# One token of gated attention plus a GLU: the first loads divided over two issue queues

## The chip, the cores and the metric

The kernel runs on one core of a Trainium2 chip. Five engines work side by side, each with its own instruction queue: TensorE (PE) for matmuls, VectorE (DVE), ScalarE (ACT), GpSimd (POOL) and SyncE (SP). Sixteen DMA engines move data between the chip's memory (HBM) and the on-chip memory of 128 partitions (SBUF). A load is issued by an instruction in the queue of SP, ACT or POOL and ends by raising a semaphore. The metric is device time in microseconds (us), the median of several runs.

## The reference

One token attends to the last 4096 positions of a cache with 8 key/value heads and 32 query heads; a small network with a sigmoid runs beside it; a scalar gate mixes the two.

```python
W = min(4096, max(256, Sk // 4))               # 4096
q = (x @ wq).reshape(B, Sq, Hq, Dh)            # x: 512, wq: 512 x 4096
k, v = (last W positions of k_cache, v_cache)  # 8 heads x 4096 x 128 each
p = softmax(q . k * Dh ** -0.5)
a = (p . v).reshape(B, Sq, Hq * Dh) @ wo       # wo: 4096 x 512
h = sigmoid(x @ w_gate) * (x @ w_up)           # 512 x 1792 each
b = h @ w_down                                 # 1792 x 512
g = sigmoid((x * gate_w).sum(-1))
out = g * a + (1 - g) * b
```

All inputs are bf16. Each weight and each cache row is used once, and together they are 30.7 MB.

## The kernel before

All large loads are issued by SP in the order in which they are used: `wq_sb` (L80, 4 MB, 32 KB per partition), the four K pairs `kn` (L84 through `load_pair`, 2 MB each), `wg_sb` (L94), `wu_sb` (L99) and its remainder `wx_sb` (four small loads, L105), the four V pairs `vv`, `wo_sb` in two halves (L115) and `wd_sb` in four pieces (L120), the last of them 128 KB. A pair is two heads of the cache, and partition 2x + y of its tile holds head y's block number x. The V pairs take over the buffers of the K pairs, so that each V load waits until the K pair's transposes are done. `wo_sb` takes over the buffer of `wq_sb`.

ACT issues two small loads at the very start: x and `gate_w`, 1 KB each, into one partition of `xr` (L74, L75). At the end it issues the output (L343).

POOL makes the constants: `identf`, `ident`, `ones_f`, the zeroed `qbig`, `permT` (L123 to L134). DVE clears a scalar `spare` four times (L137), makes `other` and `selI`, and forms the gate from `xr` (gpr L165, gsum L166, then z_ps L168 on PE and gex L170 on ACT). PE turns x into a column (`xt_ps` L148, copied to `xT` L158).

From L177 on the order on PE, DVE and ACT is the order of the program text; before it, and on SP and POOL, the framework's scheduler sets it. PE first fills the score tiles with a mask (L182), then computes q, replicated over all partitions, in eight pieces of four matmuls (`q_ps` L200). ACT copies each piece (L202), DVE transposes (`qtT` L205) and places q in `qbig` (L216). For each of four pairs and two halves DVE transposes K in 32 x 32 blocks (`kT` L188) and PE adds eight matmuls to the scores (L227). Then come the maximum, the gate matmuls of the GLU (`glu(0)`), the exponential (L269), its transpose `eT` (L271), the 64 matmuls with V (`pv_ps` L299), the up matmuls (`glu(1)`), the reordering of the attention result (`oT`, `oX`, `oY`), and 92 narrow pairs' worth of matmuls with `wo_sb` and `wd_sb` that add everything into `a_ps` (`add_row`, L290). DVE and ACT copy the result (L341, L342).

The framework gives loads issued by SP and ACT eight completion semaphores in rotation. A load whose semaphore still belongs to an unfinished load waits in its queue, and everything behind it in that queue waits with it. The end of the program (L369) is a chain of waits on SP for every semaphore that is still open, and then a meeting of all engines.

Of the kernel before, what the change touches and what calls it, by code (L numbers as in the profile page):

```python
# [17 lines left out]
def kernel(  # L18
# [14 lines left out]
    nc = tc.nc  # L33

    P = 128
# [7 lines left out]
    W = min(4096, max(256, Sk // 4))  # L43
    KB = W // P
    SBASE = Sk - W
# [3 lines left out]
    NC_O = HQ * DH // P  # L49
# [5 lines left out]
    HP = Hkv // 2  # L55
    R2 = 2 * REP
    NP = 2 * KB
# [13 lines left out]


    xr = const.tile([1, 2, D], BF16, name="xr")
    nc.scalar.dma_start(xr[:, 0, :], A_x[0, :, :])  # L74
    nc.scalar.dma_start(xr[:, 1, :], gate_w.rearrange("(o n) -> o n", o=1))  # L75

    dq = nc.sync
    wq_sb = big.tile([P, DC, HQ * DH], BF16, name="wq_sb", tag="big")
    wq_v = A_wq.rearrange("(p c) n -> p c n", c=DC)
    dq.dma_start(wq_sb[:], wq_v)  # L80


    def load_pair(t, cache, a, n0=0, n1=NP):
        dq.dma_start(t[:, n0:n1, :].rearrange("p n d -> p (n d)"),  # L84
                     cache[0, 2 * a:2 * a + 2, SBASE:SBASE + W, :]
                     .rearrange("y (x n) d -> x y n d", n=NP)[:, :, n0:n1, :].rearrange("x y n d -> x y (n d)"))

    kn = []
    for a in range(HP):
        kn.append(blk.tile([P, NP, P], BF16, name="kn", tag="blk"))  # L90
        load_pair(kn[a], A_k_cache, a)

    wg_sb = w14.tile([P, DC, F], BF16, name="wg_sb", tag="w14")
    dq.dma_start(wg_sb[:], B_w_gate.rearrange("(p c) f -> p c f", c=DC))  # L94
# [13 lines left out]
    for a in range(HP):  # L108
        vv.append(blk.tile([P, NP, P], BF16, name="vv", tag="blk"))
        load_pair(vv[a], A_v_cache, a)  # L110

    wo_sb = big.tile([P, NC_O, N_OUT], BF16, name="wo_sb", tag="big")
    wo_v = A_wo.rearrange("(p c) n -> p c n", c=NC_O)
    for c0 in (0, NC_O // 2):
        dq.dma_start(wo_sb[:, c0:c0 + NC_O // 2, :], wo_v[:, c0:c0 + NC_O // 2, :])  # L115

    wd_sb = w14.tile([P, NJ, N_OUT], BF16, name="wd_sb", tag="w14")
    wd_v = B_w_down.rearrange("(p j) n -> p j n", j=NJ)
    for j0, j1 in zip(WD_SPLIT[:-1], WD_SPLIT[1:]):
        dq.dma_start(wd_sb[:, j0:j1, :], wd_v[:, j0:j1, :])  # L120


    identf = const.tile([P, P], F32, name="identf")  # L123
# [9 lines left out]
    nc.gpsimd.tensor_copy(permT[:].rearrange("p (k j) -> p k j", j=4),  # L133
                          ident[:].rearrange("p (j k) -> p k j", j=4))  # L134
    spare = const.tile([1, 1], F32, name="spare")
    for _ in range(4):
        nc.vector.memset(spare[:], 0.0)  # L137

    other = const.tile([2, HQ * 4 // R2, 2, REP], BF16, name="other")
# [234 lines left out]
```

## Time and profile before

| quantity | value |
|---|---|
| median of 6 runs | 80.47 us (80.29 to 80.73) |
| the profiled execution | 80.44 us, of which 78.8 us span |
| busy PE, DVE, ACT, POOL | 53.7, 38.9, 10.8, 3.3 us |
| HBM read | 30.67 MB, 389 GB/s over the span |
| x's first consumer (DVE L153, PE L148) | 2.04 to 2.06 us |
| gate_w's consumer (DVE L165) | 8.01 us |
| first query matmul (L200) | 13.34 us |
| last load's first consumer (L290) | 75.62 us |
| mean granted TensorE clock | 0.957 |

The slices of the page divide the span into 40 equal parts; a digit is a busy share in tenths. The chain is read backwards from the last instruction: what released it, what released that, and so on. A waits line gives who waited for whom, with the total, the number of times and the longest. A windows line gives the stretch and its length, then the busy time and number of instructions of PE, its weight loads, DVE, ACT and POOL, then the granted clock, the mean share of the 16 DMA engines and GB/s. In a window that is shorter than a packet's time the DMA figures count the packets that begin in it, so that a share can exceed 1.

### The profile page before, as it was taken

Reading aid. Unit: us, or ns where it says so; the run is one execution under the profiler, and the core shown is the slowest. Engines: PE = TensorE matmul, PEld = TensorE weight load, DVE = VectorE, ACT = ScalarE, POOL = GpSimd, SP = SyncE. Lnnn points to the kernel's source line nnn. Section 1 sums busy time; section 2 is a strip of 40 time slices with the busy share of each in tenths; the row PEclk is TensorE's granted clock in tenths of the full one; section 3 lists DMA queues with packets and bytes.
Section 4 is the critical chain, followed back from the end, with each engine's and each line's share of the span. In section 5 each row is a group of like instructions: output and inputs, shape, how many; then the busy total and the mean of one; then the engine's idle time right before and its main releaser. Section 6 shows DMA issues by size and latency. Waiting matters only on the chain.

```text
span 78.8 us, 798 instructions
## 1 busy us (share of the span) xinstructions
PE 53.7 (68%) x314; PEld 24.1 (31%) x314; DVE 38.9 (49%) x52; ACT 10.8 (14%) x20; POOL 3.3 (4%) x10
## 2 busy tenths in 40 slices
PE   0200093999960999988889511999998799566750
PEld 0200041333410334433333110344442345345520
DVE  1600920009739999999995618994000000690020
ACT  2400000233763000000000257000000002000010
POOL 7900000000000000000000000000000000000000
PEclk9999999999999579999999999569999999999999
DMA  5889988999999999999999999999999999999710
GB/s 150 299 349 516 433 383 374 416 466 433 416 416 449 441 408 416 447 400 440 396 444 426 416 416 458 433 424 399 424 449 441 416 408 441 428 383 414 284 38 1
DMA packets 2616, 30.71 MB, mean 390 GB/s; under 512 B 307, under 2 KB 438, under 8 KB 822
## 3 DMA queue, kind: packets, MB, share of 16 engines
q1 hardware_dynamic: 2608, 30.67, 92.7%
q8 instruction: 2, 0.03, 0.2%
q10 hardware_dynamic: 6, 0.00, 0.0%
HBM read 30.67 MB, written 0.00 MB: 389 GB/s over the span
## 4 chain that ended last, share of the span: by engine, by line
DMA 76%; PE 13%; DVE 6%; ACT 1%; issue 0%
DMA wd_sb<-in_B_w_down_dram 36%; DMA vv<-in_A_v_cache_dram 24%; DMA wq_sb<-in_A_wq_dram 16%; PE q_ps L200 12%; DVE kT L188 3%; DVE qbig L216 2%; DVE qtT L205 1%; PE a_ps L290 1%; ACT q_sb L202 1%; DVE res L341 1%
## 5 line engine op out<-in xcount | busy, mean ns | idle before, releaser
L227 PE MATMUL S_ps<-kT,qbig 128*128 128x512 bf16 x64 | 16.3, 406 | 3.9 <-DVE qbig L216 2.8
L188 DVE STREAM_TRANSPOSE kT<-kn 128x2048 f32<-128x2048 f32 x8 | 17.8, 2279 | 0.0
L299 PE MATMUL pv_ps<-vv,eT 128*32 128x512 bf16 x64 | 15.2, 411 | 3.6 <-DVE eT L271 2.8
L227 PEld LDWEIGHTS <-qbig 128*128 128x128 bf16 x64 | 6.5, 103 | 13.7 <-issue 4.4
L200 PE MATMUL q_ps<-wq_sb,xT 128*128 128x512 bf16 x32 | 9.6, 475 | 1.4 <-DMA wq_sb<-in_A_wq_dram 1.4
L299 PEld LDWEIGHTS <-eT 128*32 128x32 bf16 x64 | 6.0, 103 | 11.9 <-issue 3.6
L205 DVE STREAM_TRANSPOSE qtT<-q_sb 128x512 f32<-128x512 f32 x4 | 2.8, 701 | 7.9 <-ACT q_sb L202 7.9
L318 DVE TENSOR_TENSOR oT<-o_ps,rb 128x32 bf16<-128x32 f32 x1 | 0.2, 191 | 12.1 <-PE o_ps L316 12.1
L200 PEld LDWEIGHTS <-xT 128*128 128x128 bf16 x32 | 3.8, 118 | 7.6 <-issue 5.5
L182 PE MATMUL S_ps<-ident,other 2*128 2x512 bf16 x4 | 2.0, 611 | 5.9 <-DVE other L140 5.9
L202 ACT CAST q_sb<-q_ps 128x512 bf16<-128x512 f32 x8 | 4.7, 585 | 8.0 <-PE q_ps L200 8.0
L290 PE MATMUL a_ps<-wo_sb,oY 128*1 128x256 bf16 x64 | 3.8, 272 | 1.7 <-DMA wo_sb<-in_A_wo_dram 1.4
L290 PEld LDWEIGHTS <-oY 128*1 128x1 bf16 x64 | 2.7, 83 | 3.3 <-issue 1.6
L271 DVE STREAM_TRANSPOSE eT<-e_sb 128x1024 bf16<-128x1024 bf16 x2 | 2.4, 1224 | 1.9 <-ACT e_sb L269 1.9
L254 ACT ACTIVATE sge<-gu_ps 128x448 f32<-128x448 f32 x1 | 0.5, 543 | 18.9 <-PE gu_ps L243 18.9
L165 DVE TENSOR_TENSOR gpr<-xr 1x512 f32<-1x512 bf16 x1 | 0.7, 679 | 4.7 <-DMA xr<-in_gate_w_dram 4.7
L341 DVE CAST res<-a_ps 1x256 bf16<-1x256 f32 x1 | 0.4, 412 | 5.2 <-PE a_ps L290 5.2
L281 DVE RECIPROCAL sg<-sge 128x448 f32<-128x448 f32 x1 | 3.0, 2953 | 0.0
L309 ACT COPY pv_sb<-pv_ps 128x512 f32<-128x512 f32 x1 | 0.6, 585 | 16.6 <-PE pv_ps L299 16.6
L249 DVE TENSOR_REDUCE pm<-S_ps 128x1 f32<-128x1024 f32 x2 | 2.4, 1204 | 0.9 <-PE S_ps L227 0.9
L148 PE MATMUL xt_ps<-ident,xr 1*128 1x1 bf16 x4 | 0.3, 165 | 3.5 <-POOL ident L126 3.5
L290 PE MATMUL a_ps<-wd_sb,hT 128*1 128x256 bf16 x28 | 2.0, 271 | 0.7 <-DMA wd_sb<-in_B_w_down_dram 0.7
(62 smaller groups left out, 31.0 us busy)
## 6 DMA issues: line engine op xcount, KB each, us to landing
kn<-in_A_k_cache_dram SPq DMA_DIRECT2D x4, 2048.0 KB, 27.5
vv<-in_A_v_cache_dram SPq DMA_DIRECT2D x4, 2048.0 KB, 18.8
wq_sb<-in_A_wq_dram SPq DMA_DIRECT2D x1, 4096.0 KB
wo_sb<-in_A_wo_dram SPq DMA_DIRECT2D x2, 2048.0 KB
wg_sb<-in_B_w_gate_dram SPq DMA_DIRECT2D x1, 1792.0 KB
wu_sb<-in_B_w_up_dram SPq DMA_DIRECT2D x1, 1456.0 KB
wd_sb<-in_B_w_down_dram SPq DMA_DIRECT2D x1, 1024.0 KB
wd_sb<-in_B_w_down_dram SPq DMA_DIRECT2D x1, 384.0 KB
```

What stands on the lines that cost most here:

```text
L182: nc.tensor.matmul(S_ps[u // 2][:, u % 2, :], lhsT=other[:].rearrange("p o y u -> p (o y u)"), rhs=ident[0:2, 0:2].rearrange("p (o y) -> p ...
L188: nc.vector.transpose(t[:].bitcast(F32), kn[a][:, v * KB:(v + 1) * KB, :] .rearrange("p n d -> p (n d)").bitcast(F32))
L200: nc.tensor.matmul(q_ps[:], lhsT=xT[:, c:c + 1].to_broadcast([P, P]), rhs=wq_sb[:, c, ks], start=(c == 0), stop=(c == DC - 1))
L202: nc.scalar.copy(q_sb[:, ks], q_ps[:])
L205: nc.vector.transpose(qtT[:].bitcast(F32)[:, kq], q_sb[:].bitcast(F32)[:, kq])
L216: copy(q_dst[rows, :, 32 * qd:32 * qd + R2, :, t], q_src[rows, :, :, :, 0, t])
L227: nc.tensor.matmul(S_ps[v][:, hb, :], lhsT=q_st[:, a, dhi, :, t], rhs=k_v[:, hb * 16:(hb + 1) * 16, dhi, :, t], start=False, stop=(a == HP ...
L249: nc.vector.tensor_reduce(pm2[:, v:v + 1], S_ps[v][:].rearrange("p a b -> p (a b)"), axis=AX.X, op=ALU.max)
L271: nc.vector.transpose(eT[:, :, v * KB:(v + 1) * KB, :].rearrange("p a n r -> p n a r"), e_sb[:, v, :].rearrange("p (n a r) -> p n a r", a= ...
L281: nc.vector.reciprocal(sg[:], sge[:])
L290: nc.tensor.matmul(a_ps[32 * i:32 * i + 1, i, 0:HN], lhsT=lhsT, rhs=rhs[:, i * HN:(i + 1) * HN], start=start, stop=stop)
L299: nc.tensor.matmul(pv_ps[32 * a:32 * a + 32, :, :], lhsT=eT[:, a, 4 * m:4 * m + 4, :].rearrange("p n r -> p (n r)"), rhs=vv[a][:, 4 * m:4 ...
```

## The change

The load of `wq_sb` becomes two: the even partitions by SP's queue, the odd ones by ACT's. The first three K pairs are divided in the same way, which sends the one head of a pair by SP and the other by ACT; the fourth stays whole on SP, like everything behind it. x and `gate_w` are issued by GpSimd instead of ACT. SP gets a no-operation behind its last load, which depends on the last eight loads in the list. DVE clears `spare` twice instead of four times.

```diff
     xr = const.tile([1, 2, D], BF16, name="xr")
-    nc.scalar.dma_start(xr[:, 0, :], A_x[0, :, :])
-    nc.scalar.dma_start(xr[:, 1, :], gate_w.rearrange("(o n) -> o n", o=1))
+    nc.gpsimd.dma_start(xr[:, 0, :], A_x[0, :, :])
+    nc.gpsimd.dma_start(xr[:, 1, :], gate_w.rearrange("(o n) -> o n", o=1))
 
     dq = nc.sync
+    loads = []
+    queues = (dq, nc.scalar)
     wq_sb = big.tile([P, DC, HQ * DH], BF16, name="wq_sb", tag="big")
     wq_v = A_wq.rearrange("(p c) n -> p c n", c=DC)
-    dq.dma_start(wq_sb[:], wq_v)
+
+    for y, queue in enumerate(queues):
+        queue.dma_start(wq_sb[y:P:2], wq_v[y:P:2])
 
     def load_pair(t, cache, a, n0=0, n1=NP):
-        dq.dma_start(t[:, n0:n1, :].rearrange("p n d -> p (n d)"),
...
+        loads.append(dq.dma_start(t[:, n0:n1, :].rearrange("p n d -> p (n d)"),
...
     for a in range(HP):
         kn.append(blk.tile([P, NP, P], BF16, name="kn", tag="blk"))
-        load_pair(kn[a], A_k_cache, a)
+        if a == HP - 1:
+            load_pair(kn[a], A_k_cache, a)
+            continue
+        for y, queue in enumerate(queues):
+            queue.dma_start(kn[a][y:P:2, :, :].rearrange("p n d -> p (n d)"),
+                            A_k_cache[0, 2 * a + y, SBASE:SBASE + W, :].rearrange("(x n) d -> x (n d)", n=NP))
...
-        dq.dma_start(wo_sb[:, c0:c0 + NC_O // 2, :], wo_v[:, c0:c0 + NC_O // 2, :])
+        loads.append(dq.dma_start(wo_sb[:, c0:c0 + NC_O // 2, :], wo_v[:, c0:c0 + NC_O // 2, :]))
...
-        dq.dma_start(wd_sb[:, j0:j1, :], wd_v[:, j0:j1, :])
+        loads.append(dq.dma_start(wd_sb[:, j0:j1, :], wd_v[:, j0:j1, :]))
+
+    seen = dq.nop()
+    for load in loads[-8:]:
+        tc.add_manual_dep(seen.ins, load.ins.name,
+                          mybir.DependencyInfo(mybir.DependencyClass.Sync, mybir.DependencyReason.DATA), reason="loads ended")
...
     spare = const.tile([1, 1], F32, name="spare")
-    for _ in range(4):
+    for _ in range(2):
         nc.vector.memset(spare[:], 0.0)
```

More of the change, by code (lines that the diff above doesn't have):

```diff
@@ L73 @@
     xr = const.tile([1, 2, D], BF16, name="xr")
-    nc.scalar.dma_start(xr[:, 0, :], A_x[0, :, :])
-    nc.scalar.dma_start(xr[:, 1, :], gate_w.rearrange("(o n) -> o n", o=1))
+    nc.gpsimd.dma_start(xr[:, 0, :], A_x[0, :, :])
+    nc.gpsimd.dma_start(xr[:, 1, :], gate_w.rearrange("(o n) -> o n", o=1))
     dq = nc.sync
+    loads = []
+    queues = (dq, nc.scalar)
     wq_sb = big.tile([P, DC, HQ * DH], BF16, name="wq_sb", tag="big")
     wq_v = A_wq.rearrange("(p c) n -> p c n", c=DC)
-    dq.dma_start(wq_sb[:], wq_v)
+    for y, queue in enumerate(queues):
+        queue.dma_start(wq_sb[y:P:2], wq_v[y:P:2])
     def load_pair(t, cache, a, n0=0, n1=NP):
-        dq.dma_start(t[:, n0:n1, :].rearrange("p n d -> p (n d)"),
-                     cache[0, 2 * a:2 * a + 2, SBASE:SBASE + W, :]
-                     .rearrange("y (x n) d -> x y n d", n=NP)[:, :, n0:n1, :].rearrange("x y n d -> x y (n d)"))
+        loads.append(dq.dma_start(t[:, n0:n1, :].rearrange("p n d -> p (n d)"),
+                                  cache[0, 2 * a:2 * a + 2, SBASE:SBASE + W, :]
+                                  .rearrange("y (x n) d -> x y n d", n=NP)[:, :, n0:n1, :].rearrange("x y n d -> x y (n d)")))
     kn = []
```

## The prediction

> **What bounds the kernel now.** I read the page's slices first, then its DMA queues, the chain of work that ended last, and at last the waits and windows around the two ends of the load stream.
>
> ```profile
> PE   0200093999960999988889511999998799566750
> DVE  1600920009739999999995618994000000690020
> DMA  5889988999999999999999999999999999999710
> GB/s 150 299 349 516 433 383 374 416 466 433 416 416 449 441 408 416 447 400 440 396 444 426 416 416 458 433 424 399 424 449 441 416 408 441 428 383 414 284 38 1
> q1 hardware_dynamic: 2608, 30.67, 92.7%
> q8 instruction: 2, 0.03, 0.2%
> q10 hardware_dynamic: 6, 0.00, 0.0%
> ...
> DMA 76%; PE 13%; DVE 6%; ACT 1%; issue 0%
> ```
>
> The DMA row stands at 9 from the fourth or fifth slice to the 37th: the 16 engines are full while PE and DVE have holes. The 30.67 MB of q1 fill 92.7% of 78.8 us, 73.0 us on each engine. So the end is the start of the load stream, plus 73 us, plus what follows the last load.
>
> The chain in order of time says the same of the end:
>
> ```profile
> 0.73 12.56 DMA wq_sb<-in_A_wq_dram
> 13.34 9.61 PE q_ps L200 x32
> ...
> 28.07 18.81 DMA vv<-in_A_v_cache_dram
> 46.90 28.68 DMA wd_sb<-in_B_w_down_dram
> 75.62 0.64 PE a_ps L290 x6
> 76.26 0.40 DVE res L341
> ```
>
> The last load is consumed from 75.62 us on; 0.64 us of matmuls, the 0.40 us copy, the output's transfer and the closing waits make 3.2 us up to 78.8. The profiled run took 80.44 us, so 1.64 us lie outside the span; the median is 80.47, 0.03 above. The piece at 28.07 is a V load waiting in line behind other loads, not an idle queue.
>
> Compute has little slack against the loads, in four waits (the last line is from SP's own waits; columns: who for whom, us in total, times, longest):
>
> ```profile
> PE q_ps L200 <- DMA wq_sb<-in_A_wq_dram: 1.4, 1, 1.4
> PE pv_ps L299 <- DMA vv<-in_A_v_cache_dram: 0.9, 1, 0.9
> PE a_ps L290 <- DMA wo_sb<-in_A_wo_dram: 1.4, 1, 1.4
> PE a_ps L290 <- DMA wd_sb<-in_B_w_down_dram: 0.7, 2, 0.5
> DVE gpr L165 <- DMA xr<-in_gate_w_dram: 4.7, 1, 4.7
> SPq L105 <- DMA wq_sb<-in_A_wq_dram: 8.3, 1, 8.3
> ```
>
> The reader is to see two numbers here: 1.4 us before the query matmuls, and 0.9 + 1.4 + 0.7 = 3.0 us later, which a late compute chain can eat before the end moves.
>
> The start, in narrow windows (columns: window, busy of the engines, clock, DMA share, GB/s booked where a packet starts):
>
> ```profile
> 0.00:1.70 1.70, 0.00 (x0) 0.00 (x0) 0.24 (x4) 0.18 (x1) 1.15 (x8) 1.00 0.00 1
> 1.70:2.10 0.40, 0.00 (x0) 0.04 (x1) 0.06 (x1) 0.40 (x1) 0.40 (x1) 1.00 3.92 1065
> 2.10:2.40 0.30, 0.00 (x0) 0.07 (x1) 0.30 (x2) 0.30 (x1) 0.30 (x1) 1.00 0.00 0
> 2.40:2.60 0.20, 0.00 (x0) 0.00 (x0) 0.20 (x2) 0.20 (x1) 0.20 (x1) 1.00 1.35 492
> ```
>
> 0.40 us x 1065 GB/s is 13 packets of 32 KB, one on each of 13 engines; 0.20 x 492 is the three others, about 0.6 us later (middles of the windows: 1.9 and 2.5). That stagger, and not a lack of queued work, is what a second queue could shorten.
>
> **The change, part by part.** *wq and three K pairs as halves on two queues.* Bytes stay (10.5 MB); five instructions' work becomes nine: SP issues one wq half, three K halves and the fourth pair; ACT four halves. Rows for one issue: 0.39 us (wq) and 0.61 to 0.74 us (K). On ACT four of them replace two small ones (0.51 and 0.21 us): its queue is busy to 0.73 + 0.39 + 3 x 0.68 = 3.2 us instead of 1.5, then its table load of 1.28 us ends at 4.5 instead of 2.8. ACT's first work is gex at 10.72; over 6 us cover it. Without them the gate chain would move one for one.
>
> The gain at the start: if a half of wq spreads over the 16 engines in half the time, the 0.6 us stagger shrinks to 0.3. Bounds: 0.6 us saved, and 0.3 lost if two queues that start together delay each other (an estimate: half of the 0.7 us by which the first packets, about 1.9 us, exceed the usual 1.21). I take -0.3, the middle of none and all of the stagger. More cannot be had here, since the stream behind runs full: DMA shares of 1.01 and 1.02 in the windows from 13.34 to 61.63. Four more loads end with 16 completion packets each, one per engine, of 9 ns: +0.04 us.
>
> [...]
>
> *Does a second queue's ring cost?* No row shows two bulk queues on one engine. The nearest are two. gate_w's 1 KB packet went between wq's packets at 6.4 us and no wq packet around it was longer: 0. The instruction fetch (two packets of 16 KB, 1.06 and 1.11 us) did cost: the V packet behind the first took 1.11 us instead of 0.61, the packet behind the second 0.76 instead of 0.31, so 0.5 us for a bulk switch. Each engine has 32 packets in the two-queue phase; alternating after every packet would make up to 32 x 0.5 = 16 us. A gain is bounded by the packets too: 32 KB take 1.213 us and twice 16 KB 2 x 0.614, so a packet costs 15 ns beside its bytes; a second ring that hid it for 32 packets would save 0.5. Ends: -0.5 and +16. I take 0, because gate_w went by a queue of the same kind as these loads (hardware_dynamic, q10) and the fetch by another (q8), and keep 16 for a rival.
>
> *Do the halves still use all 16 engines, evenly?* Nearest row: wx's loads of 32 partitions, whose packets were never more than nine in flight, mostly eight. A half on eight engines would move 10.5 MB at 213 instead of 427 GB/s: +24.6 us. Below: 0. I take 0, because wx's source is divided into eight blocks, and the halves have 64 equal rows in source and target.
>
> [...]
>
> *SP's order.* The trace shows eight completion semaphores in rotation: the ninth load reuses the first one's. That is the wait of L105 for wq above. Now the first eight are the two wq halves and six K halves, so the fourth K pair waits for wq (about 13.3 us), and wg, wu and wx, which are behind it on SP, wait each for a K half. At 13.3 us 6.3 MB are still queued, 14.8 us of work; at the thinnest point, about 26.6 us, 5.6 MB (fourth K pair, wg, wu, wx), 13 us. So 0; if that cover ran out, idle DMA time would add itself to the end. V loads wait as before for the K tiles' transposes (first at 28.07).
>
> *x and gate_w by GpSimd.* Two issues leave ACT and go ahead of POOL's seven constants. Bounds for one from ACT's rows and POOL's longest: 0.21 to 1.86 us, so `ident` is ready between 3.9 and 7.2 us instead of 3.4. The consumer is xt_ps, which then waits for x anyhow. The arrival matters more. Before, x arrived at 2.04, ahead of wq's packets, but gate_w, behind three of them, at 8.01. From there gpr, gsum, the constants and L182's matmuls take 4.0 us (8.01 to 11.99), and wq lets q_ps start at 13.34: gate_w may arrive up to 9.4 us. With two bulk rings ahead, I put x at 6.4 to 9 us, and gate_w one round of two 32 KB packets (2.5 us) after the first packet at 6.4: 8.9. Bounds 8.0 and 13.8 (three rounds). The value stays within the 1.4 us; 13.8 makes q_ps 4.4 us late, and 3.0 us of that disappear in the later waits: +1.4 at the end.
>
> *SP's no-operation* waits for the last eight loads. Behind it on SP is only the kernel's closing chain of waits, which already waits there (23.4 us for wd, with longest 21.8). With it, the output's own semaphore can be followed by few others; the closing waits after the output cost about 0.06 us each. 0, bounds -0.1 and +0.2.
>
> *Two memsets fewer on DVE*: 2 x 0.06 us and gaps, before x arrives. 0, below which nothing can come since DVE then waits for x; above, 0.35 us (selI) if the constants change places with the gate chain.
>
> **Sum:** 80.44 - 0.3 + 0.04 = 80.18 against the profiled run; with the 0.03 to the median, 80.2.
>
> **Rivals.** *Nothing moves*: the stagger stays, since all first packets end near 3.7 to 4.4 us whatever their start; 80.5. For it: full DMA rows. Against it: the last engine to finish also fixes the end.
>
> [...]
>
> *x too late*: gate_w after 12.4 us (9.4 + 3.0) moves the end; 80.5 to 82.0 (13.8 - 12.4 = 1.4 over 80.5). For it: 4.7 us waited already. Against: the three later waits.
>
> **How the numbers follow.** Tell-apart bound for this kernel: 0.3%, 0.24 us. Start gain: 0.58, its own range 79.8 to 80.8 (0.6 saved and 0.1 at the tail, or 0.3 lost), of this 0.40 faster, 0.14 same, 0.04 slower. Nothing moves: 0.12 (0.09 same, 0.03 slower). Rings or halves cost: 0.18, slower. x late: 0.12, slower. Faster 0.40, same 0.23, slower 0.37. The range goes from 79.5 (the start's 79.8 with part of the hidden 15 ns) to 82.4 (late x at its bound of 82.0, the tail's 0.2 and 0.2 more if wq lands later); it leaves out most of the ring case, 0.15, and 0.03 below.
>
> **What would show it.** Right: packets of all 16 engines before 2.3 us, DMA share near 1.0 from 4 us, the wait for wd near 75.4 us. K landings at 18, 23, 28 and 33 us as before. Wrong: a mean GB/s under 400 between 4 and 26 us (rings, halves); q_ps released by DVE and not by wq, with no wait left on wo or wd (x late); new waits on SP after the output's landing (tail); an idle DMA slice after 13 us (semaphore rotation).

## The result and the profile after

| quantity | before | after |
|---|---|---|
| median of all runs | 80.46 us (35 runs) | 80.95 us (16 runs) |
| median of the runs that the ratio uses | 80.44 us (27 runs) | 80.86 us (9 runs) |
| ratio, with its 95% interval | | 1.0051 [1.0039, 1.0063] |
| the profiled execution | 80.44 us | 80.86 us |
| its span, and what lies outside it | 78.78 + 1.66 us | 79.13 + 1.73 us |
| first packets of `wq_sb` begin | 1.75 us | 2.09 us |
| gate_w's consumer | 8.01 us | 13.89 us |
| first query matmul | 13.34 us | 17.86 us |
| last load's first consumer | 75.62 us | 75.94 us |

The change makes the kernel 0.5% slower, 0.41 us. Some executions of most versions were disturbed and took about 1.3 us or more longer; the ratios leave them out, and of the profiles of four experiments that fell in such an execution (split only, columns, adjacent blocks, no-operation only) only the first 23 us and the closing are read.

The two profiled executions differ by 0.42 us, and the table says where: 0.32 us in the moment at which the last load is consumed, 0.08 us outside the span, and the remaining 0.02 in the closing. So the question is why the load stream ends 0.32 us later. The page of the kernel after shows no hole in the stream and no lost bandwidth (slices of the DMA engines, then the queues, with packets, MB and share):

```profile
DMA  0999897999999999999999999999999999999710
...
q1 hardware_dynamic: 2352, 25.43, 76.1%
q10 hardware_dynamic: 322, 5.24, 16.3%
...
q0 software_dynamic: 64, 0.00, 0.1%
```

5.24 MB have moved to ACT's queue (q10), and the two shares, 76.1 and 16.3%, make 92.4% of 79.1 us, where q1 alone had 92.7% of 78.8 before: 73.1 us per engine against 73.0. The first slice of the DMA row has fallen from 5 to 0, though. The windows at the start show the same more finely (columns as in the prediction):

```profile
1.70:2.10 0.40, 0.00 (x0) 0.00 (x0) 0.00 (x0) 0.00 (x0) 0.40 (x2) 1.00 0.65 164
2.10:2.40 0.30, 0.00 (x0) 0.00 (x0) 0.00 (x0) 0.00 (x0) 0.30 (x2) 1.00 4.05 1092
2.40:2.60 0.20, 0.00 (x0) 0.00 (x0) 0.00 (x0) 0.00 (x0) 0.20 (x2) 1.00 0.45 164
2.60:3.60 1.00, 0.00 (x0) 0.00 (x0) 0.00 (x0) 0.34 (x1) 0.98 (x3) 1.00 0.30 98
```

The last column times the length gives the 32 KB packets that begin: 0.40 x 164 is two, 0.30 x 1092 is ten, 0.20 x 164 one, 1.00 x 98 three. Before, 13 began in the first of these windows. The stream is the same one, shifted by about a third of a microsecond.

The chain of work that ended last has a new head and the old tail:

```profile
1.84 12.02 DMA xr<-in_gate_w_dram
...
17.86 9.47 PE q_ps L215 x32
...
48.25 27.64 DMA wd_sb<-in_B_w_down_dram
75.94 0.65 PE a_ps L305 x6
76.58 0.40 DVE res L356
```

At its head stands `gate_w` instead of `wq_sb`: 12.02 us for 1 KB. The compute chain really starts 4.5 us later (q_ps at 17.86 instead of 13.34). But the tail still hangs on the load of `wd_sb`, as before. The waits say how close that was (who for whom, us in total, times, longest):

```profile
PE xt_ps L163 <- DMA xr<-in_A_x_dram: 10.9, 1, 10.9
...
DVE gpr L180 <- DMA xr<-in_gate_w_dram: 2.7, 1, 2.7
...
PE a_ps L305 <- DMA wd_sb<-in_B_w_down_dram: 0.2, 1, 0.2
```

Of the waits for loads that the kernel before had later on, the ones before `q_ps`, the V matmuls and `wo_sb` are gone. 0.2 us before the last piece of `wd_sb` is all that remains: the 4.5 us were absorbed, to within that margin. SP's own waits hold what the change does to the completion semaphores:

```profile
SPq L88 <- DMA wq_sb<-in_A_wq_dram: 8.4, 1, 8.4
```

The fourth K pair now waits for a wq half, as the prediction had it, and the full DMA row shows that it starved nothing.

### The profile page after: what moved, and what is told of

Its sections match the earlier page's. It is cut to its first block, busy times and chain, and to the rows that moved or that the text cites. A ratio compares the mean times of both kernels' runs of the same rounds, so it can differ in the third digit from the quotient of the medians.

```text
span 79.1 us, 805 instructions
## 1 busy us (share of the span) xinstructions
PE 52.3 (66%) x314; PEld 23.6 (30%) x314; DVE 37.8 (48%) x50; ACT 10.8 (14%) x20; POOL 4.4 (6%) x12
## 3 DMA queue, kind: packets, MB, share of 16 engines
q1 hardware_dynamic: 2352, 25.43, 76.1%
q10 hardware_dynamic: 322, 5.24, 16.3%
## 4 chain that ended last, share of the span: by engine, by line
DMA 50%; DVE 16%; PE 15%; issue 10%; SPq 3%; ACT 1%; POOL 1%; DVEq 0%; POOLq 0%
DMA wd_sb<-in_B_w_down_dram 35%; DMA xr<-in_gate_w_dram 15%; PE q_ps L215 12%; DVE kT L203 11%; PE S_ps L197 2%; DVE qbig L231 2%; SPq L124 1%; SPq L129 1%; DVE qtT L220 1%; DVE gpr L180 1%; DVE gsum L181 1%; PE a_ps L305 1%; ACT q_sb L217 1%; SPq L88 1%; POOL xr L74 1%
## 5 line engine op out<-in xcount | busy, mean ns | idle before, releaser
L242 PE MATMUL S_ps<-kT,qbig 128*128 128x512 bf16 x64 | 16.3, 405 | 3.9 <-DVE qbig L231 2.8
L314 PE MATMUL pv_ps<-vv,eT 128*32 128x512 bf16 x64 | 14.2, 412 | 2.8 <-DVE eT L286 2.8
L242 PEld LDWEIGHTS <-qbig 128*128 128x128 bf16 x64 | 6.4, 102 | 13.8 <-issue 4.5
L314 PEld LDWEIGHTS <-eT 128*32 128x32 bf16 x64 | 5.8, 103 | 10.3 <-DVE eT L286 2.9
L284 ACT ACTIVATE e_sb<-S_ps,nb 128x1024 bf16<-128x1024 f32 x2 | 2.2, 1109 | 0.0
```

What stands on the lines that cost most here:

```text
L242: nc.tensor.matmul(S_ps[v][:, hb, :], lhsT=q_st[:, a, dhi, :, t], rhs=k_v[:, hb * 16:(hb + 1) * 16, dhi, :, t], start=False, stop=(a == HP ...
L284: nc.scalar.activation(e_sb[:, v, :], S_ps[v][:].rearrange("p a b -> p (a b)"), AF.Exp, bias=nb[:], scale=scale, accum_out=rs2[:, v:v + 1])
L314: nc.tensor.matmul(pv_ps[32 * a:32 * a + 32, :, :], lhsT=eT[:, a, 4 * m:4 * m + 4, :].rearrange("p n r -> p (n r)"), rhs=vv[a][:, 4 * m:4 ...
```

## The experiments

Three candidates were there for the late start: that two queues which start a bulk load at the same moment delay each other; that a load of 64 partitions takes longer to issue, whatever its queue; and that x by GpSimd is at fault, by its lateness or otherwise. The issue instructions of the two kernels pointed at the second (start, us, engine, line, operation). Before:

```profile
0.73 0.39 SPq L80 DMA_DIRECT2D wq_sb<-in_A_wq_dram  x1
```

After:

```profile
0.73 0.56 SPq L84 DMA_DIRECT2D wq_sb<-in_A_wq_dram  x1
0.74 0.54 ACTq L84 DMA_DIRECT2D wq_sb<-in_A_wq_dram  x1
1.23 0.62 POOL L74 DMA_DIRECT2D xr<-in_A_x_dram  x1 [0.79 <-POOLq L373]
```

Half as many rows take 0.17 us more. But these two instructions also run side by side, so the trace alone couldn't tell the first two candidates apart.

### Only x and gate_w by GpSimd

The kernel before with this edit alone:

```diff
-    nc.scalar.dma_start(xr[:, 0, :], A_x[0, :, :])
-    nc.scalar.dma_start(xr[:, 1, :], gate_w.rearrange("(o n) -> o n", o=1))
+    nc.gpsimd.dma_start(xr[:, 0, :], A_x[0, :, :])
+    nc.gpsimd.dma_start(xr[:, 1, :], gate_w.rearrange("(o n) -> o n", o=1))
```

> The kernel before, with x and gate_w issued by GpSimd and nothing else changed. Theory S (two bulk queues that issue their first loads at the same moment slow each other, so the stream starts about 0.3 us later): SP issues wq alone in about 0.39 us, first packets near 1.75 us, last load consumed near 75.6 us, 80.3 to 80.5 us. Theory X (x's late arrival sets the end): gate_w's consumer after 12 us, q_ps near 16 to 18 us, no wait left on wo, 80.8 to 81.0 us.

Measured: 1.0026 [1.0016, 1.0037], the profiled execution 80.68 us. The load stream is untouched: `wq_sb` issues in 0.38 us, first packets at 1.75, the last load consumed at 75.62 as before. gate_w's consumer moves to 10.56 and the first query matmul to 14.47 us, and the waits for `wo_sb` (1.2 us) and `wd_sb` (0.8) stay: the lateness of x costs nothing here. The 0.24 us between the two profiled executions are elsewhere. 0.06 lie outside the span (1.72 instead of 1.66), 0.05 before the output has landed (77.87 instead of 77.82 us), and 0.13 after that, where SP goes through three closing waits in 0.19 us instead of one in 0.07, and the clearing of the semaphores takes 139 ns instead of 98.

### Only the halves

The kernel before with `wq_sb` and three K pairs divided as in the change; x stays first on ACT's queue, and there is no no-operation:

```diff
-    dq.dma_start(wq_sb[:], wq_v)
+    queues = (dq, nc.scalar)
+    for y, queue in enumerate(queues):
+        queue.dma_start(wq_sb[y:P:2], wq_v[y:P:2])
...
+        for y, queue in enumerate(queues):
+            queue.dma_start(kn[a][y:P:2, :, :].rearrange("p n d -> p (n d)"),
```

> The kernel before, with wq and three K pairs as halves on SP and ACT; x and gate_w stay first on ACT, no no-operation, four memsets. Theory S: ACT's bulk half comes behind x, 0.5 us or more after SP's, so that SP's issue meets only x as before: first packets near 1.75 us, 80.4 to 80.6 us. Theory H (halves of 64 partitions start or run worse, whatever the queue): 80.8 to 81.0 us. Theory X: gate_w is early, 80.4 to 80.6 us. Theory N (the closing waits on SP): without the no-operation the waits after the output's landing grow by 0.1 to 0.3 us.

Measured: 1.0077 [1.0054, 1.0101]. SP's half takes 0.56 us to issue and the first packets begin at 2.07 us, although ACT, which issues x and gate_w first, comes to its own half only at 1.51. The late start is there without two bulk issues side by side. This version is slower than the whole change: after the output has landed SP passes five closing waits in 0.33 us where the kernel before has one of 0.07.

### The halves on one queue

The change with both halves of everything on SP:

```diff
-    queues = (dq, nc.scalar)
+    queues = (dq, dq)
```

> The changed kernel with all halves on SP's queue, even then odd; the rest as changed. Theory S: first packets near 1.75 us or earlier, 80.4 to 80.6 us. Theory H: first packets after 2 us and 80.8 to 81.0 us. Theory X: x still comes by GpSimd and late, q_ps after 16 us, and the time stays near 80.9 us whatever the start.

Measured: 1.0044 [1.0025, 1.0062], 80.92 us in the profiled execution. The two issues of `wq_sb` stand together in the timeline, and no packet begins before 2.05 us:

```profile
0.73 1.20 SPq L84 DMA_DIRECT2D wq_sb<-in_A_wq_dram  x2
```

```profile
1.70:2.05 0.35, 0.00 (x0) 0.00 (x0) 0.00 (x0) 0.32 (x1) 0.35 (x2) 1.00 0.00 0
```

One queue, 0.56 and 0.58 us for the two issues, first packets at 2.09, last load consumed at 75.99. That two queues delay each other falls; the load of 64 rows stands. gate_w's consumer is at 9.77 us here and the first query matmul at 13.68, 4.2 us earlier than after the change, and the last load is no earlier for it: the lateness of x isn't what moves the end.

### Without the no-operation

```diff
-    seen = dq.nop()
-    for load in loads[-8:]:
-        tc.add_manual_dep(seen.ins, load.ins.name,
...
```

> The changed kernel without SP's no-operation. Theories S, X and H: the stretch from the output's landing to the end changes by less than 0.1 us or grows by up to 0.3 us, 80.9 to 81.2 us. Theory N (the no-operation costs the difference): 80.4 to 80.6 us.

Measured: 1.0136 [1.0068, 1.0205], with 81.25 us as the fastest of six. Five closing waits after the output take 0.32 us, against one of 0.07 with the no-operation, so it is worth 0.25 us in this kernel. The interval is wide because of something else, which the profiled execution (81.89 us) shows in PE's timeline:

```profile
70.43 5.32 PE L299 MATMUL a_ps<-wo_sb,oY 128*1 128x256 bf16 x64 [0.28 <-DVE oY L333]
```

The matmuls with `wo_sb` take 5.32 us, against 3.66 in the profile after, since the granted clock falls to half from 70.5 to 73.9 us, and no wait for `wo_sb` or `wd_sb` is left. Here the compute chain sets the end: the margin of 0.2 us that the late gate_w leaves is too small for a lowered clock. That the no-operation has a part in the clock isn't shown, and the last experiment, which has it, shows the same 5.32 us.

### wq whole, the rest as changed

```diff
-    for y, queue in enumerate(queues):
-        queue.dma_start(wq_sb[y:P:2], wq_v[y:P:2])
+    dq.dma_start(wq_sb[:], wq_v)
```

> The changed kernel with wq in one load of 128 partitions on SP; the three K pairs stay halved over SP and ACT, x by GpSimd, the no-operation stays. Theory H (a half over every second partition takes longer to issue and starts the stream late): SP's first issue back at 0.39 us, first packets at 1.75 us, last load consumed near 75.6 to 75.8 us, 80.5 to 80.7 us (the late gate_w leaves the compute chain little slack). Theory S (two queues issuing together): ACT's K half is still issued at 0.73 us, so first packets stay near 2.07 us and the time near 80.9 us.

Measured: 80.58 and 80.72 us, too few runs for an interval. The issues:

```profile
0.73 0.54 ACTq L98 DMA_DIRECT2D kn<-in_A_k_cache_dram  x1
0.73 0.39 SPq L83 DMA_DIRECT2D wq_sb<-in_A_wq_dram  x1
```

Side by side in the same 0.4 us, the 128-row load takes 0.39 and the 64-row load 0.54 us. First packets are back at 1.76 us, and the last load is consumed at 75.81, 0.13 earlier than after the change. The start gives 0.33, of which 0.2 are lost again on the way: 74.05 us from the first packets to the last consumer, where six other profiles (before, after, x by GpSimd, one queue, x on ACT, columns with x on ACT) have 73.8 to 73.9. Where they are lost isn't known.

### x back on ACT, the rest as changed

```diff
-    nc.gpsimd.dma_start(xr[:, 0, :], A_x[0, :, :])
-    nc.gpsimd.dma_start(xr[:, 1, :], gate_w.rearrange("(o n) -> o n", o=1))
+    nc.scalar.dma_start(xr[:, 0, :], A_x[0, :, :])
+    nc.scalar.dma_start(xr[:, 1, :], gate_w.rearrange("(o n) -> o n", o=1))
```

> The changed kernel with x and gate_w back on ACT, ahead of its halves. Theory H plus closing waits: stream start stays at 2.07 us and the last load's consumer at 75.9 us, gate_w's consumer before 11 us, waits on wo and wd come back, the closing is 0.1 us shorter than with GpSimd's two semaphores; 80.75 to 80.85 us. Theory X (the late x costs the difference): 80.4 to 80.5 us.

Measured: 1.0033 [1.0018, 1.0048], median 80.70 us. gate_w's consumer is at 5.60 us, and now PE waits for `wq_sb`:

```profile
PE q_ps L215 <- DMA wq_sb<-in_A_wq_dram: 4.8, 1, 4.8
```

The compute chain has all its slack back and more, and the kernel is still slower than before, with first packets at 2.08 and the last load consumed at 75.98 us. So 0.27 of the 0.41 us are there without GpSimd, and 0.14 are left for GpSimd, though the two intervals overlap.

### wq halved by columns

Each queue brings all 128 partitions, 16 KB of each:

```diff
-        queue.dma_start(wq_sb[y:P:2], wq_v[y:P:2])
+        queue.dma_start(wq_sb[:, 2 * y:2 * y + 2, :], wq_v[:, 2 * y:2 * y + 2, :])
```

> The changed kernel with wq divided by columns instead of partitions: each queue loads 16 KB of all 128 partitions. If the step over partitions or the 64 rows make the issue long: first issue 0.4 to 0.5 us, first packets 1.75 to 1.9 us, 80.5 to 80.7 us. If any second load issued at the same moment does it: first packets at 2.07 us, 80.9 us.

Measured: 1.0019 [1.0004, 1.0034], median 80.64 us. The issues:

```profile
0.74 0.38 SPq L84 DMA_DIRECT2D wq_sb<-in_A_wq_dram  x1
0.74 0.40 ACTq L84 DMA_DIRECT2D wq_sb<-in_A_wq_dram  x1
```

Again two bulk issues at the same moment, and as quick as the single one before; first packets at 1.74 us, in the window that is empty with the halves on one queue:

```profile
1.70:2.05 0.35, 0.00 (x0) 0.00 (x0) 0.00 (x0) 0.00 (x0) 0.35 (x2) 1.00 2.23 468
```

The same bytes on the same two queues start in time when they go to 128 rows. Most of the loss is gone.

### wq halved into adjacent blocks

Partitions 0 to 63 by SP, 64 to 127 by ACT:

```diff
-        queue.dma_start(wq_sb[y:P:2], wq_v[y:P:2])
+        queue.dma_start(wq_sb[64 * y:64 * y + 64], wq_v[64 * y:64 * y + 64])
```

> The changed kernel with wq divided into partitions 0 to 63 (SP) and 64 to 127 (ACT). If 64 rows make the issue long: first packets at 2.07 us. If the step of two partitions does: 1.75 us. [...]

Measured: 1.1235 [1.1199, 1.1271], about 10 us. The issues take 0.57 and 0.58 us and the first packets begin at 2.09, as with even and odd rows: the step between the rows isn't what makes an issue longer. The 10 us are something else. Of this kernel:

```profile
4.00:20.00 16.00, 0.57 (x6) 0.45 (x6) 0.33 (x2) 0.69 (x1) 1.43 (x3) 1.00 1.04 230
```

The same window of the kernel after:

```profile
4.00:20.00 16.00, 4.83 (x18) 2.14 (x19) 2.70 (x11) 0.99 (x3) 1.42 (x3) 1.00 1.01 433
```

The engines are equally full (1.04 and 1.01) and move half as much: the 128 packets of wq take 2.37 us in the median instead of 1.21. With eight of them per engine, 1.16 us more for each make 9.3 us. The late gate_w comes out of the same slow packets: its consumer is at 22.71 us instead of 13.89, so that the compute chain is late by nearly as much as the stream, and which of the two sets the end isn't settled. Why two loads of adjacent blocks are this slow isn't shown. Even and odd partitions, as many rows on the same two queues, show no such loss: 433 GB/s in this window after the change, and the whole load of 128 partitions had 417 in the kernel before.

### wx in adjacent blocks of 64

The prediction's nearest row for halves was `wx_sb`, whose four loads of 32 partitions run on eight engines. The kernel before with two loads of 64 adjacent partitions on 16 engines, in natural order, and x's copy for it likewise:

```diff
-    wx_v = B_w_up.rearrange("(h b j i c) f -> h b i j c f", h=2, b=2, j=4, i=8)[:, :, :, :, DC - 1, F - FX:F]
+    wx_v = B_w_up.rearrange("(h q c) f -> h q c f", h=2, q=64)[:, :, DC - 1, F - FX:F]
...
-        for b in range(2):
-            dq.dma_start(wx_sb[32 * b:32 * b + 32, h, :], wx_v[h, b])
+        dq.dma_start(wx_sb[:, h, :], wx_v[h])
```

> The kernel before, with wx loaded as two loads of 64 partitions in natural row order instead of four of 32 in a permuted order (x's remainder column permuted to match); nothing else. The packets of the kernel before let eight engines end near 75.0 to 75.4 us and the others near 73.4 to 74.2; if that is wx on eight engines (16 x 107 ns = 1.7 us each), spreading it over sixteen ends the loads 0.5 to 0.8 us earlier and gives 79.7 to 80.0 us. If wx's packets lie beside other work or the slow engines are slow for another reason, 80.4 to 80.5 us; 64 adjacent partitions could also collide for its 0.34 MB, at most +0.8 us.

Measured: 1.0256 [1.0230, 1.0283], 2.1 us slower, and my expectation was wrong. wx's packets take 201 ns in the median instead of 107, and the whole window moves less:

```profile
39.00:43.00 4.00, 3.71 (x27) 1.50 (x28) 3.12 (x3) 0.00 (x0) 0.00 (x0) 1.00 1.03 275
```

275 GB/s, where the kernel before has 420 in the same window:

```profile
39.00:43.00 4.00, 3.66 (x16) 1.45 (x15) 3.30 (x3) 0.00 (x0) 0.00 (x0) 1.00 1.02 420
```

145 GB/s less over 4 us are an estimated 1.4 us of the stream, and SP passes three closing waits in 0.19 us instead of one in 0.07. The rest isn't traced. The engines don't end closer together, as I had expected: the packets of the last load begin over 2.3 us, from 75.3 to 77.6 us, where they began over 2.4, from 73.0 to 75.4, and the last load is consumed at 77.79 instead of 75.62 us.

### Only the no-operation

The kernel before with the no-operation and its eight dependences:

```diff
+    seen = dq.nop()
+    for load in loads[-8:]:
+        tc.add_manual_dep(seen.ins, load.ins.name,
...
```

> The kernel before with SP's no-operation alone. In the kernel before the output's semaphore is already the last but one that SP waits for, so nothing is behind it: 80.4 to 80.5 us. If the no-operation itself costs, 80.6 us or more.

Measured: 1.0005 [0.9995, 1.0015]. It is worth nothing here, where the output's semaphore is the last in the chain anyhow. The 0.25 us that it took off stood in the changed kernel, where four more loads have shifted the rotation of the semaphores.

### wq halved by columns, x on ACT

```diff
-    nc.gpsimd.dma_start(xr[:, 0, :], A_x[0, :, :])
+    nc.scalar.dma_start(xr[:, 0, :], A_x[0, :, :])
...
-        queue.dma_start(wq_sb[y:P:2], wq_v[y:P:2])
+        queue.dma_start(wq_sb[:, 2 * y:2 * y + 2, :], wq_v[:, 2 * y:2 * y + 2, :])
```

> The changed kernel with wq halved by columns over SP and ACT, and x and gate_w back on ACT ahead of its loads. If the changed kernel's loss is the late start of 64-row loads (0.3 us) plus the closing with GpSimd's semaphores (0.15 us) and nothing else, both are gone and the two queues are worth nothing: first packets 1.75 us, 80.4 to 80.5 us. If two queues cost something of their own: 80.6 us or more; if they gain: 80.2 us or less.

Measured: 1.0020 [1.0009, 1.0031]; the profiled execution, 80.42 us, is as quick as before, with first packets at 1.75 and the last load consumed at 75.56 us. 0.1 to 0.2 us remain in the ratio of which this profile shows nothing. What they are stays open. The same halves with x by GpSimd had 1.0019: in this pair GpSimd costs nothing that can be told, where it cost 0.21 us in the kernel before. So the parts don't simply add up.

### Only the K pairs halved, with the no-operation

The change with wq whole on SP and x, gate_w on ACT, so that the K halves, the no-operation and the two memsets are left of it:

```diff
-    nc.gpsimd.dma_start(xr[:, 0, :], A_x[0, :, :])
+    nc.scalar.dma_start(xr[:, 0, :], A_x[0, :, :])
...
-    for y, queue in enumerate(queues):
-        queue.dma_start(wq_sb[y:P:2], wq_v[y:P:2])
+    dq.dma_start(wq_sb[:], wq_v)
```

> The changed kernel with wq whole on SP and x and gate_w back on ACT: of the change, the three halved K pairs, the no-operation and the memsets are left. If the loss is the 64-row first load plus GpSimd, nothing is left of it: first packets 1.75 us, 80.4 to 80.5 us. If two queues or halved K loads cost something behind the start: 80.6 us or more, with the stream's last load later than 75.62 us though it starts at 1.75.

Measured: 1.0011 [0.9998, 1.0025], the profiled execution 80.41 us, the issue of `wq_sb` 0.39 us, first packets at 1.75. Nothing is left of the loss that can be told from no change. So 64-row loads, of which this kernel has six, cost nothing that can be told behind the first load, where the stream has work queued; the interval leaves room for 0.2 us. In this profile the compute chain sets the end: the first query matmul waits for `wq_sb` until 16.1 us, 2.8 us longer than before, with packets of ACT's K half from 5.9 us on among those of wq, which end at 15.1 us instead of 13.0; and at the end no wait for a load is left.

## Why the prediction was right or wrong

**The gain at the start (-0.3 us): wrong, and in its sign.** This is the step that failed. It measured +0.32 us. Its premise, that half of wq spreads over the 16 engines in half the time, doesn't hold: a half takes 0.54 to 0.58 us to issue at the head of its queue where the whole takes 0.37 to 0.39, and its first packet comes 1.35 us after the issue begins instead of 1.02. Nor did the stagger shrink to 0.3 us: the last three of the first sixteen packets begin after 2.60 us, over 0.5 us behind the first. I read the 0.6 us stagger between the first packets and took it for a thing that scales with the load; I had no row for a 64-row load and should have seen that a first instruction of a new shape sits on the path with its whole length. The bound of +0.3 was right in size, but for a reason that the runs refute: the halves on one queue start as late, and two simultaneous 128-row halves start in time. All fourteen kernels agree on the rows: the six that begin with 64 rows of wq start at 2.07 to 2.09 us, the eight that begin with 128 at 1.73 to 1.76.

**Four more completion packets (+0.04):** not resolved by itself. From the first packets to the last consumer it is 73.87 us before and 73.85 after, so it was 0 within what the trace tells.

**The second ring (0):** right. Packets of 32 KB take 1.21 us and of 16 KB 0.61 on both queues, with both in use, so the instruction fetch was the wrong neighbour for that price, and gate_w's free passage the right one. The +16 us kept against it, and the case in which the rings cost, fall.

**All 16 engines (0):** right for even and odd rows, with 433 GB/s over 4 to 20 us. Two adjacent blocks of as many rows had 230 GB/s in that window and took about 10 us longer, so the number of rows alone doesn't decide it.

**SP's order and the eight semaphores (0):** right; the wait for wq is 8.4 us and starves nothing.

**x and gate_w by GpSimd (0):** the value for gate_w was wrong, the slack behind it too, and the conclusion held by luck. gate_w arrived at 13.89 us, past my upper bound of 13.8 and far from the 8.9 that I took. q_ps came 4.5 us late, with the 1.4 us before it already used up, and the prediction had 3.0 us of later waits against that: by its own sum the end would have moved by 13.89 - 12.4 = 1.5 us. It moved no further than the load stream did. The waits gave 2.8 us (0.2 remain), and the last load itself came 0.3 us later. The other 1.4 us are slack that the waits didn't show. 1.0 of it lies in the V stage, from the first matmul of L299 (before) or L314 (after) to the first up matmul: PE is busy for 14.41 us there before and for 13.40 after, at a granted clock of 0.89 and 0.87. So the clock isn't the reason, and the reason stays open. The rival "x too late" is that near: in the profile of the kernel without the no-operation, with its lowered clock, it decides. The sum also lacked GpSimd's part in the closing. The profiles in which x goes by GpSimd have 1.71 to 1.73 us outside the span, and those with x on ACT 1.63 to 1.67 (the kernel with only the halves is an exception with 1.82). That is the 0.08 us outside the span.

**The no-operation (0) and the memsets (0):** right in the sum. By itself the no-operation takes back 0.25 us of closing waits, which the new order of semaphores would have added; my bound of +0.2 was for something else, and I hadn't seen that the change needs it.

So, of the 0.41 us, the 64-row first load has 0.3 by the profiles (the shift of the stream) and 0.1 to 0.3 by the ratios of three pairs of kernels that differ in it alone: 0.26 (the change, 1.0051, against wq by columns, 1.0019), 0.18 (x on ACT, 1.0033, against only the K pairs, 1.0011) and 0.10 (x on ACT against columns with x on ACT, 1.0020). GpSimd has 0.21 in the kernel before, 0.14 in the changed one and nothing with the columns. The K halves, the second queue and the no-operation have nothing that can be told from 0. The rival "nothing moves" had the right answer for the second queue and the K halves, but its reason, that the start of the first packets doesn't matter, falls: of their shift of 0.34 us, 0.32 came through to the end. No version that ran is faster than the kernel before.

## What to carry to other kernels

Where a kernel is a full stream of loads from its first packet to its last, the end can move with the first packet (0.34 us at the start became 0.32 at the end here), so that the issue time of the very first load is on the path, while dividing the loads behind it cost nothing that could be told (1.0011 [0.9998, 1.0025] with the K pairs alone); look for a row of the same shape before a load is divided there. Dividing a load over two queues brought nothing where the DMA engines were full (73.87 us from the first packets to the last consumer before, 73.85 after), and dividing it into adjacent instead of alternating rows took the bandwidth from 433 to 230 GB/s over 4 to 20 us. Four more loads also shifted the rotation of completion semaphores here and with it the waits that close the program: read the end of the trace too. And slack that is added up from the waits of a trace isn't the whole of it: the chain made up 1.4 us more than its waits showed.

## What the runs showed of the hardware

- A load of `wq_sb` with 64 partitions took longer to issue (0.50 to 0.58 us) than one with 128 and as many or twice as many bytes (0.36 to 0.40), with rows a step of two apart or adjacent, on SP or ACT, alone or beside another. Rows aren't all that counts, since the whole K pairs, 128 partitions from two heads, took 0.61 to 0.74. Why isn't settled.
- Two 64-row loads of adjacent blocks, in flight together on two queues, wrote 230 GB/s; two of even and odd rows 433.
- 1 KB into one partition, from the start of its issue to its consumer: gate_w took 8.7 us by GpSimd beside one bulk queue (1.85 to 10.56) and 12.0 beside two (1.84 to 13.89), by ACT 6.7 beside one (1.28 to 8.01) and 4.3 beside two (1.26 to 5.60). GpSimd's load came as 16 pieces of 64 bytes and 16 completion packets of 4 bytes, 64 packets for x and gate_w in q0, spread from 7.6 to 13.5 us after the change.
- Each closing wait on SP takes about 0.065 us, five of them 0.32 to 0.33.
